# Layer 0's product with w_out: weight columns move, intermediates stand; its output in token rows

## The chip, the cores and the metric

One core of one Trainium2 chip runs the whole program. The metric is device time in microseconds (us), as the median of three runs. The engines are PE (matrix products; its weight loads are listed apart as PEld), DVE and ACT (element-wise work), POOL (element-wise work that can't read PSUM) and SP, whose queue issues nearly all DMA transfers. They run side by side, each in its own fixed order, and wait for each other by semaphores.

## What is computed

Causal attention with a forget bias for 4 x 8 heads of 576 tokens, then two feed-forward layers over the 2304 tokens. Model width is 512, inner width 2048.

```python
attn_out = _attn_ref(**attn_kwargs)                      # [4, 8, 576, 64]
x = attn_out.transpose(0, 2, 1, 3).reshape(B * S, H * D)  # [2304, 512]

# layer 0
h = x @ w_in
r = np.maximum(h, 0.0)
g = s * (r * r) + b          # s, b: one number each
x = g @ w_out

# layer 1
h = x @ w_in
g = np.maximum(h, 0.0) + alpha * np.minimum(h, 0.0)
return g @ w_out
```

Since b is one number, b's part of layer 0's result is b times the column sums of w_out, the same row for every token. The kernel calls it `bsum`.

## The kernel before

**Precision.** Every operand of a matmul is split into a high and a low part (`split`, L129: ACT copies the source rounded, DVE or POOL subtracts). A product is three matmuls: high x high, high x low, low x high. The weights come as 64-bit numbers and are rebuilt to 32 bits by one ACT and two DVE instructions (`convert`, L134) before they are split.

**Blocks.** Tokens go in blocks of T = 256. `SIZES` (L621) gives layer 0 seven narrow blocks of 256 tokens (t = 0 to 6) and a wide one of 512 (t = 7). Layer 1 has one narrow block (t = 0) and then four wide ones. A block is 16 steps f, one for each 128 of the inner width. `up(f)` (L699) makes 128 inner values for all its tokens: 12 matmuls into `hp`, the weights stationary, the tokens moving. ACT, DVE or POOL then make the high and low part `gh` and `gl` (in wide blocks and in layer 1 they lie in `ring`, `gl`'s part written at L131). `down(f)` (L740) multiplies by w_out and adds into the accumulators `acc`. `down` runs 2 steps behind `up` in layer 0 and 3 behind in layer 1 (`LAG`). `finish` (L761) takes the accumulators out through `res`.

**The two forms of down.** In layer 0 (L746) a 128x128 piece of w_out is stationary and `gh` or `gl` moves: 4 pieces x 3 terms = 12 matmuls a step, of 256 columns in a narrow block and 512 in the wide one. The result has the model's columns on the partitions and tokens along the row, as `up` of the next layer needs it. In layer 1 (L756) 128 tokens of `gh` or `gl` are stationary and the 512 columns of w_out move: 3 matmuls for each 128 tokens, 6 a step in the narrow block and 12 in a wide one. The result has tokens on the partitions, as the output needs it.

**Between the layers.** Layer 0's `finish` scales and adds `bsum` (L772, L776: a bias for each partition) and stores to the DRAM tile `x2_d`, which keeps the turned form. `inputs(1, t)` loads it as it lies (L636 for the narrow block, L657 for wide ones: 4 loads of 256 KB) and splits it. `sum_columns` (L233) makes `bsum` with 32 matmuls near the end of layer 0's first block, when all its weights are there.

**Attention** runs beside layer 0's narrow blocks. It is cut into units; `pace` says how many units must be done by which step, and the units' pieces are issued between the steps. Its loads of q and k (L323) bring pieces of 32 columns (128 B) to 32 partitions each, and DVE turns every 32x32 square (`nc.vector.transpose`, L371).

**Order.** Within the program order as written a scheduler moves instructions on each engine by its own estimate of times. SP's queue is in order, and at most 8 of its transfers are on the way at once.

Of the kernel before, what the change touches and what calls it, by code (L numbers as in the profile page):

```python
# [19 lines left out]
def tile_forget_attention__then__two_mlps(  # L20
# [597 lines left out]
    x2_d = dram.tile([NB, P, NCC * T], F32, name="x2_d")  # L618
# [3 lines left out]
    BLOCKS = [(layer, t) for layer in range(2) for t in range(len(SIZES[layer]))]  # L622

    def inputs(layer, t):
# [4 lines left out]
        if layer == 0:  # L629
            src = xf.pop(t)  # L630
            xh = one.tile([P, NCC, T], F32R, tag=f"xh{t % 2}", name=f"xh{layer}_{t}")
            xl = one.tile([P, NCC, T], F32R, tag=f"xl{t % 2}", name=f"xl{layer}_{t}")
            xh, xl = ([x[:, c] for c in range(NCC)] for x in (xh, xl))
        else:
            src = one.tile([P, NCC, T], F32, tag="res", name=f"x2_{t}")
            nc.sync.dma_start(out=src, in_=x2_d[t].rearrange("p (c n) -> p c n", n=T))  # L636

            xh, xl = (
                [
                    two.tile([P, T], F32R, tag=tag, name=f"x{tag}{layer}_{t}_{c}", bufs=3 if c < 3 else 2)  # L640
                    for c, tag in enumerate(tags)
                ]
                for tags in (("gh", "gh", "gh", "r"), ("gl", "gl", "gl", "r"))
            )
        for c in range(NCC):
            on_pool = layer == 0 and t
            split(xh[c], xl[c], src[:, c], nc.gpsimd if on_pool else nc.vector)
        return xh, xl

    def wide_inputs(layer, t, first):  # L650
        xh, xl = [], []
        src = []
        for half in range(2):
            if layer == 1:
                src.append(xfp.tile([P, 2, 2, T], F32, tag="xf", name=f"x2_{t}_{half}"))
                for z in range(2):
                    nc.sync.dma_start(  # L657
                        out=src[half][:, :, z],
                        in_=x2_d[first + z, :, half * 2 * T : (half + 1) * 2 * T].rearrange("p (c n) -> p c n", n=T),
                    )  # L660
# [14 lines left out]
        for c in range(NCC):  # L675
            if layer == 1:
                split(xh[c], xl[c], src[c // 2][:, c % 2].rearrange("p z n -> p (z n)"))
# [9 lines left out]
    def mlp_block(layer, t, x):  # L687
# [52 lines left out]
        def down(f, g):  # L740
            w = packet(layer, f)
            if layer == 0:
                terms = ((w[2], g[0]), (w[3], g[0]), (w[2], g[1]))
                for d in range(NCC):
                    for n, (a, b) in enumerate(terms):
                        nc.tensor.matmul(  # L746
                            banks[d] if count == 2 else acc[d // 2][:, d % 2], a[:, d * P : (d + 1) * P], b,
                            start=(f == 0 and (d % 2 == 0 or count == 2) and n == 0),
                            stop=(f == NF - 1), skip_group_check=True,
                        )  # L750
            else:
                gh, gl = g
                _, _, woh, wol = w
                for m in range(TB // P):
                    for a, b in ((gh, woh), (gh, wol), (gl, woh)):
                        nc.tensor.matmul(  # L756
                            banks[m], a[:, m * P : (m + 1) * P], b,
                            start=(f == 0 and b is woh and a is gh), stop=(f == NF - 1 and a is gl),
                        )

        def finish():  # L761
            for m, bank in enumerate(banks):
# [4 lines left out]
                if layer == 0:  # L767
                    for z in range(1 if count == 2 else 2):
                        d = m if count == 2 else 2 * m + z
                        dst, src = (res, bank) if count == 2 else (x[:, z * T : (z + 1) * T] for x in (res, bank))  # L770
                        if d % 2:
                            nc.scalar.activation(  # L772
                                dst, src, AF.Identity, scale=gate_s[:, 0:1], bias=bsum[:, d : d + 1]
                            )
                        else:
                            nc.vector.tensor_scalar(  # L776
                                out=dst, in0=src, scalar1=gate_s[:, 0:1], scalar2=bsum[:, d : d + 1],
                                op0=ALU.mult, op1=ALU.add,
                            )
                elif m % 2:  # L780
                    nc.scalar.mul(res, bank, 1.0 / W_SCALE)
                else:
                    nc.vector.tensor_scalar(out=res, in0=bank, scalar1=1.0 / W_SCALE, scalar2=None, op0=ALU.mult)
                if layer == 0 and count == 2:
                    nc.sync.dma_start(
                        out=x2_d[first : first + 2, :, m * T : (m + 1) * T].rearrange("z p n -> p z n"),
                        in_=res.rearrange("p (z n) -> p z n", n=T),
                    )
                elif layer == 0:
                    nc.sync.dma_start(out=x2_d[t, :, m * 512 : (m + 1) * 512], in_=res)  # L790
                else:
                    p0 = first * T + m * P
                    nc.sync.dma_start(out=out[p0 : p0 + P, :], in_=res)
# [98 lines left out]
```

## Time and profile before

| | |
|---|---|
| runs | 1047.58, 1049.14, 1053.61 us |
| median | 1049.14 us |
| span of the profiled execution | 1046.3 us |
| PE busy, matmuls | 1031.2 us, 6376 |
| PEld busy | 910.3 us |
| DVE busy | 584.2 us |
| ACT busy | 625.9 us |
| POOL busy | 340.6 us |
| mean DMA rate | 80 GB/s |

The profile is of one execution. Its span runs from the first to the last instruction and lies a little under the times of the runs. PE's busy time says little, since matmuls are pipelined and their ends are modelled; the distance from one start to the next, or a count in a stretch, says more. The stages of the span are: attention with the weights' arrival and layer 0's first block (to about 170 us), attention beside layer 0's other narrow blocks (to about 556), layer 0's wide block, in which layer 1's weights are loaded and converted (to about 650), layer 1's narrow block (to 689), and its wide blocks.

### The profile page before, as it was taken

What the parts mean: (1) busy time and instruction counts of PE and PEld (TensorE: products, weight loads), DVE (VectorE), ACT (ScalarE), POOL (GpSimd) and SP (SyncE); (2) the same over time, 40 slices, a digit from 0 to 9 for tenths busy, and PEclk for the clock granted to TensorE, in tenths of its full rate; (3) what the DMA queues carried; (4) which work ended last, traced back from release to release, by engine and by line L of the source; (5) the groups of instructions that cost most, each with busy time, mean ns of one, the idle gap of its engine ahead of it and who ended that gap; (6) DMA issues with size and microseconds to landing.
All of it is one profiled execution on the core that took longest, in us unless ns stands there. A gap on an engine that the chain in (4) does not pass through costs nothing.

```text
span 1046.3 us, 18413 instructions
## 1 busy us (share of the span) xinstructions
PE 1031.2 (99%) x6376; PEld 910.3 (87%) x6376; DVE 584.2 (56%) x1437; ACT 625.9 (60%) x1493; POOL 340.6 (33%) x752
## 2 busy tenths in 40 slices
PE   9899999999999999999999999999999999999998
PEld 4578899999999999999998888988888888888887
DVE  6789776687667766767655766532223224222222
ACT  5778766877787877878776766542334324333232
POOL 5344565766677566777550000000000000000000
PEclk9899999999999999999999999999999999999999
DMA  6998433243133332324215742300002002001001
GB/s 133 241 236 247 129 76 72 71 96 78 39 89 70 95 79 44 86 63 90 63 54 178 243 162 88 94 21 1 1 1 81 1 1 81 1 0 41 1 1 41
DMA packets 173470, 83.36 MB, mean 80 GB/s; under 512 B 135552, under 2 KB 160896, under 8 KB 173376
## 3 DMA queue, kind: packets, MB, share of 16 engines
q1 hardware_dynamic: 171984, 81.94, 29.8%
q8 instruction: 50, 0.82, 0.3%
q10 hardware_dynamic: 1392, 0.24, 0.1%
q14 instruction: 44, 0.36, 0.1%
HBM read 72.63 MB, written 9.51 MB: 79 GB/s over the span
## 4 chain that ended last, share of the span: by engine, by line
PE 84%; DVE 6%; DMA 3%; issue 2%; ACT 2%; SPq 2%; POOL 1%; DVEq 0%; POOLq 0%; ACTq 0%
PE hp L710 35%; PE acc L756 19%; PE acc L746 17%; PE pt L511 4%; PE av L527 4%; PE sc L456 2%; PE sc L455 1%; DMA wo<-in_moe_w_out_dram 1%; DVE probs L431 1%; SPq L323 1%; PE sc L453 1%; DVE probs L457 1%; DVE wt L142 1%; DMA cum<-cum_d 1%; PE colsum L241 1%
## 5 line engine op out<-in xcount | busy, mean ns | idle before, releaser
L710 PE MATMUL hp<-xh,w 128*128 128x256 f32 (+1 forms) x1536 | 397.3, 330 | 2.3 <-ACT r L729 1.5
L710 PEld LDWEIGHTS hp<-xh,w 128*128 128x128 f32 x1536 | 267.5, 189 | 31.1 <-ACT r L729 1.8
L710 PE MATMUL hp<-xl,w 128*128 128x256 f32 (+1 forms) x768 | 252.7, 329 | 0.3 <-DVE xl L131 0.3
L729 ACT ACTIVATE r<-hp 128x256 f32<-128x256 f32 (+1 forms) x208 | 96.5, 464 | 226.3 <-PE hp L710 214.7
L756 PE MATMUL acc<-w,ring 128*128 128x512 f32 x864 | 209.0, 390 | 0.0
L756 PEld LDWEIGHTS acc<-w,ring 128*128 128x128 f32 x864 | 161.3, 188 | 33.3
L746 PE MATMUL acc<-gh,w 128*128 128x256 f32 x896 | 169.9, 286 | 0.4 <-ACT res L772 0.3
L734 DVE SCALAR_TENSOR_TENSOR r<-u,misc,r 128x512 f32<-128x512 f32 (+1 forms) x80 | 55.8, 698 | 200.5 <-ACT u L733 200.5
L710 PEld LDWEIGHTS hp<-xl,w 128*128 128x128 f32 x768 | 145.2, 189 | 13.2 <-DVE xl L131 0.5
L746 PEld LDWEIGHTS acc<-gh,w 128*128 128x128 f32 x896 | 135.3, 189 | 2.9 <-ACT res L772 1.0
L746 PE MATMUL acc<-gl,w 128*128 128x256 f32 x448 | 117.6, 287 | 2.0 <-POOL gl L131 2.0
L480 POOL TENSOR_SCALAR probs<-probs,sm 64x64 f32<-64x64 f32 (+4 forms) x160 | 91.9, 587 | 63.7 <-DVE sm L477 56.4
L469 ACT ACTIVATE probs<-probs,nm 64x64 f32<-64x64 f32 (+4 forms) x160 | 90.0, 563 | 32.4 <-DVE nm L457 26.8
L131 POOL TENSOR_TENSOR gl<-r,gh 128x256 fp32r<-128x256 f32 x112 | 89.2, 797 | 61.8 <-ACT gh L130 55.6
L131 DVE TENSOR_TENSOR ring<-r,ring 128x512 fp32r<-128x512 f32 (+1 forms) x96 | 62.1, 647 | 60.9 <-ACT ring L130 60.9
L457 DVE CUSTOM_DVE_ANT_0 probs<-sc,probs 128x320 f32<-128x320 f32 (+3 forms) x160 | 68.3, 428 | 44.6 <-PE sc L456 31.4
L130 ACT CAST ring<-r 128x512 fp32r<-128x512 f32 (+1 forms) x96 | 56.0, 584 | 53.3 <-DVE r L734 52.7
L746 PEld LDWEIGHTS acc<-gl,w 128*128 128x128 f32 x448 | 79.8, 188 | 3.4 <-POOL gl L131 2.6
L511 PE MATMUL pt<-ident,probs 128*128 128x128 f32 x480 | 76.2, 278 | 2.8 <-POOL probs L480 2.8
L545 DVE TENSOR_TENSOR xf<-av,xf 64x128 f32<-64x128 f32 (+3 forms) x88 | 28.0, 318 | 67.7 <-ACT xf L544 67.2
L511 PEld LDWEIGHTS pt<-ident,probs 128*128 128x128 f32 x480 | 55.5, 141 | 9.4 <-POOL probs L480 4.4
L431 DVE TENSOR_SCALAR probs<-cum,cumT 64x64 f32<-64x64 f32 (+4 forms) x137 | 57.5, 468 | 5.6 <-issue 2.0
(116 smaller groups left out, 1557.8 us busy)
## 6 DMA issues: line engine op xcount, KB each, us to landing
wi<-in_moe_w_in_dram SPq DMA_DIRECT2D x32, 512.0 KB, 5.1
wo<-in_moe_w_out_dram SPq DMA_DIRECT2D x32, 512.0 KB, 4.9
cum<-cum_d SPq DMA_DIRECT2D x32, 288.0 KB, 3.5
cum<-cum_d SPq DMA_DIRECT2D x30, 160.0 KB, 3.1
nat<-in_k_dram SPq DMA_DIRECT2D x64, 72.0 KB, 2.5
x_d<-res SPq DMA_DIRECT2D x18, 256.0 KB, 2.2
out_dram<-res SPq DMA_DIRECT2D x18, 256.0 KB, 2.1
vn<-in_v_dram SPq DMA_DIRECT2D x32, 128.0 KB, 2.9
```

Of the source, the lines that this page charges most:

```text
L130: nc.scalar.copy(hi, src)
L131: lo_eng.tensor_tensor(out=lo, in0=src, in1=hi.bitcast(F32), op=ALU.subtract)
L431: nc.vector.tensor_scalar(out=pt[:rows, :i1], in0=u.cums[h][:rows, :i1], scalar1=cumT[:rows, r, head : head + 1], scalar2=0.0, op0=ALU.sub ...
L457: nc.vector.tensor_tensor_reduce(out=pt[:rows, j0:j1], in0=scr, in1=pt[:rows, j0:j1], scale=SCALE if flip else -SCALE, scalar=init, op0=AL ...
L469: nc.scalar.activation(pt[:rows, :n], pt[:rows, :n], AF.Exp, bias=nm[:rows, m : m + 1], scale=1.0 if flip else -1.0, accum_out=sm[:rows, m ...
L480: nc.gpsimd.tensor_scalar(out=probs[r][:rows, :n], in0=probs[r][:rows, :n], scalar1=sm[:rows, m : m + 1], scalar2=1.0, op0=ALU.mult, op1=A ...
L511: nc.tensor.transpose(tp[:, o : o + P], u.probs[h][r][:, k0 : k0 + P], ident)
L710: nc.tensor.matmul(hs, a[:, c], b[c], start=(n == 0), stop=(n == len(terms) * NCC - 1))
L729: relus.append(nc.scalar.activation(r, hs, AF.Relu, scale=1.0 / W_SCALE).ins)
L734: nc.vector.scalar_tensor_tensor(out=r, in0=u, scalar=nalpha[:, f : f + 1], in1=r, op0=ALU.mult, op1=ALU.add)
L746: nc.tensor.matmul(banks[d] if count == 2 else acc[d // 2][:, d % 2], a[:, d * P : (d + 1) * P], b, start=(f == 0 and (d % 2 == 0 or count ...
L756: nc.tensor.matmul(banks[m], a[:, m * P : (m + 1) * P], b, start=(f == 0 and b is woh and a is gh), stop=(f == NF - 1 and a is gl),)
```

## The change

Layer 0's `down` takes layer 1's form: `gh` and `gl` are stationary, w_out's 512 columns move. `finish` becomes one for both layers, with only a scale, and `x2_d` holds token rows. `inputs(1, t)` brings them back to the turned form: `load_rows` loads pieces of 32 columns with the pattern of q and k, 4 loads for each 128 columns, DVE turns the 32x32 squares, and `split_biased` adds `bsum` while it splits. A narrow block's load is 16 transfers in place of 1, a wide one's 16 in place of 4.

```diff
-    x2_d = dram.tile([NB, P, NCC * T], F32, name="x2_d")
+    x2_d = dram.tile([NT, DM], F32, name="x2_d")
+    def load_rows(dst, t0, n, c):
+
+        for g in range(4):
+            nc.sync.dma_start(
+                out=dst[32 * g : 32 * (g + 1)].rearrange("p (b d) -> p b d", d=32),
+                in_=x2_d[t0 : t0 + n, c * P + 32 * g : c * P + 32 * (g + 1)].rearrange("(b p) d -> p b d", p=32),
+            )
+
+    def split_biased(hi, lo, src, c):
+        nc.scalar.activation(hi, src, AF.Identity, bias=bsum[:, c : c + 1])
+        nc.vector.scalar_tensor_tensor(
+            out=lo, in0=src, scalar=bsum[:, c : c + 1], in1=hi.bitcast(F32), op0=ALU.add, op1=ALU.subtract
+        )
...
-            src = one.tile([P, NCC, T], F32, tag="res", name=f"x2_{t}")
-            nc.sync.dma_start(out=src, in_=x2_d[t].rearrange("p (c n) -> p c n", n=T))
+            rows = one.tile([P, NCC, T], F32, tag="res", name=f"x2_{t}")
+            for c in range(NCC):
+                load_rows(rows[:, c], first * T, T, c)
...
+            turned = one.tile([P, T], F32, tag=("ql00", "ql10", "ql11")[c % 3], name=f"x2t_{t}_{c}")
+            nc.vector.transpose(turned, rows[:, c])
+            split_biased(xh[c], xl[c], turned, c)
...
-                src.append(xfp.tile([P, 2, 2, T], F32, tag="xf", name=f"x2_{t}_{half}"))
-                for z in range(2):
-                    nc.sync.dma_start(
-                        out=src[half][:, :, z],
-                        in_=x2_d[first + z, :, half * 2 * T : (half + 1) * 2 * T].rearrange("p (c n) -> p c n", n=T),
-                    )
+                rows = xfp.tile([P, 4 * T], F32, tag="xf", name=f"x2_{t}_{half}")
+                for c in range(2):
+                    load_rows(rows[:, c * 2 * T : (c + 1) * 2 * T], first * T, 2 * T, 2 * half + c)
+                src.append(rows)
...
-                split(xh[c], xl[c], src[c // 2][:, c % 2].rearrange("p z n -> p (z n)"))
+                if c % 2 == 0:
+                    turned = xfp.tile([P, 4 * T], F32, tag="xf", name=f"x2t_{t}_{c}")
+                    nc.vector.transpose(turned, src[c // 2])
+                split_biased(xh[c], xl[c], turned[:, c % 2 * 2 * T : (c % 2 + 1) * 2 * T], c)
...
-            w = packet(layer, f)
-            if layer == 0:
-                terms = ((w[2], g[0]), (w[3], g[0]), (w[2], g[1]))
-                for d in range(NCC):
-                    for n, (a, b) in enumerate(terms):
-                        nc.tensor.matmul(
-                            banks[d] if count == 2 else acc[d // 2][:, d % 2], a[:, d * P : (d + 1) * P], b,
-                            start=(f == 0 and (d % 2 == 0 or count == 2) and n == 0),
-                            stop=(f == NF - 1), skip_group_check=True,
-                        )
...
+            gh, gl = g
+            _, _, woh, wol = packet(layer, f)
+            for m in range(TB // P):
+                for a, b in ((gh, woh), (gh, wol), (gl, woh)):
+                    nc.tensor.matmul(
+                        banks[m], a[:, m * P : (m + 1) * P], b,
+                        start=(f == 0 and b is woh and a is gh), stop=(f == NF - 1 and a is gl),
+                    )
...
+                scale = gate_s[:, 0:1] if layer == 0 else 1.0 / W_SCALE
+                if m % 2:
+                    nc.scalar.mul(res, bank, scale)
                 else:
-                    nc.vector.tensor_scalar(out=res, in0=bank, scalar1=1.0 / W_SCALE, scalar2=None, op0=ALU.mult)
...
+                    nc.vector.tensor_scalar(out=res, in0=bank, scalar1=scale, scalar2=None, op0=ALU.mult)
+                p0 = first * T + m * P
+                nc.sync.dma_start(out=(x2_d if layer == 0 else out)[p0 : p0 + P, :], in_=res)
```

Three places show what the scheduler makes of it. The first is PE in layer 0's narrow block 3, at the down of step 4 (w_4_2_18 and w_4_2_17 are the high and low part of w_out there; pt, sc and av are attention). Before:

```order
L746 MATMUL acc_3_0_4704<-gh_3_4_5018,w_4_2_18_912 128x256
L746 MATMUL acc_3_0_4704<-gh_3_4_5018,w_4_2_17_913 128x256
L746 MATMUL acc_3_1_4705<-gh_3_4_5018,w_4_2_18_912 128x256
L746 MATMUL acc_3_1_4705<-gh_3_4_5018,w_4_2_17_913 128x256
L511 MATMUL pt_0_2_1_0_4852<-ident,probs_1_0_1_4741 128x128 x3
L455 MATMUL sc_1_0_2_2_0_4862<-xs_2_2_0_4774 128x192
L456 MATMUL sc_1_0_2_2_0_4862<-xs_2_2_0_4774,ql_113 128x192
```

After:

```order
L765 MATMUL acc_3_0_4424<-w_4_2_18_912,gh_3_4_4712 128x512
L765 MATMUL acc_3_0_4424<-w_4_2_17_913,gh_3_4_4712 128x512
L765 MATMUL acc_3_1_4425<-w_4_2_18_912,gh_3_4_4712 128x512
L765 MATMUL acc_3_1_4425<-w_4_2_17_913,gh_3_4_4712 128x512
L765 MATMUL acc_3_0_4424<-w_4_2_18_912,gl_3_4_4713 128x512
L765 MATMUL acc_3_1_4425<-w_4_2_18_912,gl_3_4_4713 128x512
L730 MATMUL hp_3_6_4916<-xh_3_4067,w_6_0_24_1233 128x256
```

The twelve of the step, of which the first four stand above, became six, and the two with `gl`, which POOL writes last, stand at their end.

The second is DVE in layer 1's narrow block, around steps 4 to 8 (r and ring belong to a step's intermediates; x_1 and x_2 are the next two wide blocks' inputs in two halves each). Before:

```order
L734 SCALAR_TENSOR_TENSOR r_0_5_10175<-u_0_5_10176,misc,r_0_5_10175 128x256
L131 TENSOR_TENSOR xl_2_0_10813<-x_2_0_10809,xh_2_0_10812 128x512 x2
L131 TENSOR_TENSOR ring_9986<-r_0_5_10175,ring_9982 128x256
L734 SCALAR_TENSOR_TENSOR r_0_6_10201<-u_0_6_10202,misc,r_0_6_10201 128x256
L131 TENSOR_TENSOR xl_2_1_10818<-x_2_1_10814,xh_2_1_10817 128x512 x2
L131 TENSOR_TENSOR ring_9987<-r_0_6_10201,ring_9983 128x256
```

After (x2t is the turned form):

```order
L131 TENSOR_TENSOR ring_9323<-r_0_5_9512,ring_9319 128x256
L696 STREAM_TRANSPOSE x2t_2_9683<-x_1_1_9666 128x1024
L754 SCALAR_TENSOR_TENSOR r_0_6_9538<-u_0_6_9539,misc,r_0_6_9538 128x256
L634 SCALAR_TENSOR_TENSOR xl_1_1_9676<-x2t_2_9683,misc,xh_1_1_9675 128x512 x2
L754 SCALAR_TENSOR_TENSOR r_0_7_9564<-u_0_7_9565,misc,r_0_7_9564 128x256
L131 TENSOR_TENSOR ring_9324<-r_0_6_9538,ring_9320 128x256
L131 TENSOR_TENSOR ring_9325<-r_0_7_9564,ring_9321 128x256
L696 STREAM_TRANSPOSE x2t_0_10184<-x_2_0_10162 128x1024
L754 SCALAR_TENSOR_TENSOR r_0_8_9590<-u_0_8_9591,misc,r_0_8_9590 128x256
L634 SCALAR_TENSOR_TENSOR xl_2_0_10172<-x2t_0_10184,misc,xh_2_0_10171 128x512 x2
L131 TENSOR_TENSOR ring_9322<-r_0_8_9590,ring_9318 128x256
```

The work on x_2 moved from steps 5 and 6 to steps 8 and 9, and the turn of its first half stands ahead of r and ring of step 8. Its loads use the buffers that the turns of x_1 free.

The third is ACT in layer 0's first block, between steps 2 and 4 (wt_7, wt_8: weight packets being rebuilt; w_6, w_7: split; probs and pf: attention). Before:

```order
L469 ACTIVATE probs_1_1_0_986,sm_1_1_0_985<-probs_1_1_0_986,nm_1_1_0_984 128x448
L130 CAST gh_0_2_1218<-r_2_1220 128x256
L130 CAST w_7_0_28_1285<-wt_7_0_1277 128x512
L515 COPY pf_0_1_1_0_1006<-pt_0_0_0_1_1001 128x512
L469 ACTIVATE probs_1_1_0_986,sm_1_1_0_985<-probs_1_1_0_986,nm_1_1_0_984 128x576
L427 ACTIVATE probs_1_1_1_1045<-cum_0_1_1_973,cumT 128x448
L427 ACTIVATE probs_1_1_1_1045<-cum_0_1_1_973,cumT 128x576
L729 ACTIVATE r_3_1272<-hp_0_3_1257 128x256
L140 ACTIVATE wt_8_0_1329<-wi_8_1241 128x512
L140 ACTIVATE wt_8_1_1333<-wo_8_1242 128x512
```

After:

```order
L469 ACTIVATE probs_1_1_0_986,sm_1_1_0_985<-probs_1_1_0_986,nm_1_1_0_984 128x448
L130 CAST w_7_0_28_1279<-wt_7_0_1271 128x512
L749 ACTIVATE r_3_1266<-hp_0_3_1251 128x256
L140 ACTIVATE wt_8_0_1317<-wi_8_1241 128x512
L140 ACTIVATE wt_8_1_1321<-wo_8_1242 128x512
L130 CAST w_7_2_30_1283<-wt_7_1_1275 128x512
L751 ACTIVATE r_3_1266<-r_3_1266 128x256
L515 COPY pf_0_1_1_0_1006<-pt_0_0_0_1_1001 128x512
L427 ACTIVATE probs_1_1_1_1045<-cum_0_1_1_973,cumT 128x448
L427 ACTIVATE probs_1_1_1_1045<-cum_0_1_1_973,cumT 128x576
```

Step 3 and packet 8 moved ahead of four pieces of attention; DVE's order changed alike, up to packet 14.

## Rows read from the trace of the kernel before

**Rows 1.** Page, busy time, share of the span and instructions of each engine.

```profile
PE 1031.2 (99%) x6376; PEld 910.3 (87%) x6376; DVE 584.2 (56%) x1437; ACT 625.9 (60%) x1493; POOL 340.6 (33%) x752
```

**Rows 2.** Stretches: us, busy PE PEld DVE ACT POOL (count), clock, DMA share, GB/s.

```profile
50.00:100.00 50.00, 47.21 (x299) 38.18 (x299) 46.13 (x107) 39.22 (x94) 22.34 (x33) 1.00 0.94 252
300.00:350.00 50.00, 50.00 (x420) 49.94 (x419) 35.71 (x114) 40.26 (x117) 36.70 (x90) 1.00 0.33 74
720.00:1020.00 300.00, 300.00 (x1322) 247.81 (x1321) 88.06 (x124) 101.53 (x179) 0.00 (x0) 1.00 0.05 18
```

**Rows 3.** Chain of waits, narrow block, layer 0: start us, us, what, instructions.

```profile
402.75 1.66 PE acc L746 x14
...
442.74 1.43 PE hp L710 x12
```

**Rows 4.** PE by form, layer 0's down: count, busy us, mean ns, idle before.

```profile
L746 PE MATMUL acc<-gh,w 128*128 128x256 f32 x896 | 169.9, 286 | 0.4 <-ACT res L772 0.3
...
L746 PE MATMUL acc<-gl,w 128*128 128x256 f32 x448 | 117.6, 287 | 2.0 <-POOL gl L131 2.0
```

**Rows 5.** Chain of waits, layer 1's narrow block.

```profile
661.14 1.44 PE hp L710 x12
662.58 1.40 PE acc L756 x6
```

**Rows 6.** Chain of waits, wide blocks of layer 0 (L746) and layer 1 (L756).

```profile
606.87 2.79 PE acc L746 x12
...
726.53 2.72 PE acc L756 x12
```

**Rows 7.** Tile acc: layer 0's evictions, ns min/median/max; then who waited (us, times).

```profile
L776 DVE TENSOR_SCALAR res<-acc,misc x16: 505/530/809, 169.7 to 652.0; 128x256 f32<-128x256 f32 x14, 128x512 f32<-128x512 f32 x2
L772 ACT ACTIVATE res<-acc,misc x16: 547/558/777, 170.6 to 653.2; 128x256 f32<-128x256 f32 x14, 128x512 f32<-128x512 f32 x2
...
  PEld acc L746: 1.0, 3
  PE acc L746: 0.3, 2
```

**Rows 8.** DMA: issues with KB each and median us to landing; packets by size.

```profile
DMA packets 173470, 83.36 MB, mean 80 GB/s; under 512 B 135552, under 2 KB 160896, under 8 KB 173376
...
nat<-in_k_dram SPq DMA_DIRECT2D x64, 72.0 KB, 2.5
...
x<-x_d SPq DMA_DIRECT2D x16, 256.0 KB, 4.6
```

**Rows 9.** Line 323, SP's issue of one load of k, ns min/median/max.

```profile
L323 SPq DMA_DIRECT2D nat<-in_k_dram x112: 311/461/2185, 45.1 to 486.9; - x112
```

**Rows 10.** Lines 371, 131, 734 on DVE, ns min/median/max: turn, low part, two operations.

```profile
L371 DVE STREAM_TRANSPOSE turned<-nat x29: 823/1026/1045, 5.4 to 498.9; 128x832 f32<-128x832 f32 x16, 128x640 f32<-128x640 f32 x13
...
L131 DVE TENSOR_TENSOR xl<-x,xh x16: 684/688/694, 658.5 to 885.7; 128x512 fp32r<-128x512 f32 x16
...
L734 DVE SCALAR_TENSOR_TENSOR r<-u,misc,r x80: 474/752/756, 645.0 to 1033.0; 128x512 f32<-128x512 f32 x64, 128x256 f32<-128x256 f32 x16
```

**Rows 11.** Timeline of DVE, layer 1's narrow block, rings of steps 5 and 8.

```profile
664.23 0.42 DVE L131 TENSOR_TENSOR ring<-r,ring 128x256 fp32r<-128x256 f32 x1
...
670.01 0.43 DVE L131 TENSOR_TENSOR ring<-r,ring 128x256 fp32r<-128x256 f32 x1 [0.47 <-ACT ring L130]
```

**Rows 12.** Timeline of PE, the same block, down of step 8.

```profile
676.62 1.56 PE L756 MATMUL acc<-w,ring 128*128 128x512 f32 x6
```

**Rows 13.** Chain of waits from 60 to 110 us; line 140's waits (us, times).

```profile
76.29 6.84 DMA wi<-in_moe_w_in_dram
...
93.40 6.83 DMA wo<-in_moe_w_out_dram
...
  DMA wi<-in_moe_w_in_dram: 5.5, 5
...
  DMA wo<-in_moe_w_out_dram: 1.8, 3
```

More of the change, by code (lines that the diff above doesn't have):

```diff
@@ L645, in inputs @@
         for c in range(NCC):
-            on_pool = layer == 0 and t
-            split(xh[c], xl[c], src[:, c], nc.gpsimd if on_pool else nc.vector)
+            if layer == 0:
+                split(xh[c], xl[c], src[:, c], nc.gpsimd if t else nc.vector)
+                continue
+            turned = one.tile([P, T], F32, tag=("ql00", "ql10", "ql11")[c % 3], name=f"x2t_{t}_{c}")
+            nc.vector.transpose(turned, rows[:, c])
+            split_biased(xh[c], xl[c], turned, c)
         return xh, xl
@@ L740, in down @@
         def down(f, g):
-            w = packet(layer, f)
-            if layer == 0:
-                terms = ((w[2], g[0]), (w[3], g[0]), (w[2], g[1]))
-                for d in range(NCC):
-                    for n, (a, b) in enumerate(terms):
-                        nc.tensor.matmul(
-                            banks[d] if count == 2 else acc[d // 2][:, d % 2], a[:, d * P : (d + 1) * P], b,
-                            start=(f == 0 and (d % 2 == 0 or count == 2) and n == 0),
-                            stop=(f == NF - 1), skip_group_check=True,
-                        )
[L751 to L759, printed above, removed]
+            gh, gl = g
[6 more added lines that the diff above has]
+                    )
         def finish():
@@ L766, in finish @@
                 res = both[:, m % 2 * 512 : (m % 2 + 1) * 512]
[L767 to L781, printed above, removed]
-                else:
-                    nc.vector.tensor_scalar(out=res, in0=bank, scalar1=1.0 / W_SCALE, scalar2=None, op0=ALU.mult)
[L784 to L793, printed above, removed]
+                scale = gate_s[:, 0:1] if layer == 0 else 1.0 / W_SCALE
+                if m % 2:
+                    nc.scalar.mul(res, bank, scale)
+                else:
+                    nc.vector.tensor_scalar(out=res, in0=bank, scalar1=scale, scalar2=None, op0=ALU.mult)
+                p0 = first * T + m * P
+                nc.sync.dma_start(out=(x2_d if layer == 0 else out)[p0 : p0 + P, :], in_=res)
         return up, down, finish
```

## The prediction

> **What bounds the kernel now.** I read the page's busy times first, then the table by stretches, then the chain of waits in three places, and only then single tiles. TensorE (PE) has work for 99% of the span [rows 1], but that busy time is partly modelled, so the count of matmuls in a stretch tells more. From 300 to 350 us, inside layer 0's narrow blocks, 420 matmuls fill 50 us, and the weight loads (PEld) are busy for 49.94 of them; DVE and ACT have about 14 and 10 us free there [rows 2]. That is 0.119 us a matmul, although those of the attention move 64, 128 or 320 columns. In this stage the engine takes one stationary operand every 0.119 us, whatever moves over it: 12 up matmuls of 256 columns take 1.43 us and 14 down matmuls 1.66 us, with no other engine between them in the chain [rows 3]. In layer 1 the wide blocks run at 1322 matmuls in 300 us, PEld busy for 247.81 of them [rows 2]: with 512 columns moving, the moving side is the limit. The clock is granted in full (1.00, 2.4 GHz) in all these stretches. Only the first 150 us are different: from 50 to 100 us PE starts 299 matmuls, DVE is busy for 46.13 of 50 us and DMA moves 252 GB/s at a share of 0.94 [rows 2]. What counts, therefore, is PE's own work after about 150 us, and everything else only where it makes PE wait.
>
> **Removed and added on PE, narrow blocks.** Seven blocks of 16 steps lose 1344 down matmuls of 256 columns [rows 4] and get half as many of 512. A step's twelve cost 12 x 1.66/14 = 1.42 us, or 1.43 at the pitch of the up group [rows 3]. The new six exist in the trace already: layer 1's first block has 256 tokens, and its step is twelve ups of 256 and six downs of 512 with the intermediate stationary. There the six take 1.40 us and the twelve ups 1.44 [rows 5]. So a step goes from 1.43 to 1.40: 0.03 us, times 7 x 16 = 112 steps, is **3.4 us** less. The columns streamed are the same (12 x 256 = 6 x 512), which is why halving the matmuls gives so little. Bounds: if the ups behind the wider matmuls go at 1.44 for 1.43, 0.02 us a step or 2.2 us is left. If the six go at the pitch of the wide blocks, 2.72/2 = 1.36 [rows 6], it is 0.07 a step or 7.8 us. A loss is excluded by the rows: the slowest 512-column pitch among them, 1.40/6 = 0.233 us, is under two 256-column ones, 0.238. I take 3.4, since rows 5 show the same step, operand for operand.
>
> The Trainium skill speaks of this too. The page "TensorE: Matmul & The Clock Gate", section "Back-to-back issue gap", gives for a real kernel's stream of load and matmul pairs a sustained 131 ns a matmul at 512 columns. By that the estimate for a step's six is 0.79 us, 0.64 less than now, and for the sum 72 us less. The trace differs: 0.227 us in the longest undisturbed stream [rows 6], and the measurement decides.
>
> **The wide block of layer 0** (16 steps of twelve 512-column downs) swaps which operand is stationary. Its twelve take 2.79 us now; layer 1's wide blocks, which do what the change makes of it, 2.72 [rows 6]. 16 x 0.07 = **1.1 us**. The bounds are 0 (the pitch belongs to the place, not to the operands) and 1.1; I take 1.1, as the rows differ in just this.
>
> **Eviction.** A narrow block ends with two DVE and two ACT instructions of 256 columns (0.53 and 0.56 us each); they become one of 512 each, without the bias. PE and PEld wait for the ACT ones 1.3 us in all, five times [rows 7]. So between 0 and 1.3 us; I take 0, since the first bank comes free no sooner. The first block's eviction also no longer waits for the column sums; the sums still run on PE, so nothing is gained while PE has other work.
>
> **Loads of layer 1.** 17 loads become 80: 16 for the narrow block and 16 for each of four wide ones, in pieces of 128 B. Each wide one carries 64 KB. The nearest row is the load of k, with the same 32-column pattern: 72 KB land 2.5 us after issue [rows 8], and SP needs 0.461 us to issue one [rows 9]. Sixteen take 7.4 us to issue, and the last lands near 10 us, where four loads of 256 KB landed 4.6 us after issue each [rows 8]. On SP only the stores of results are queued behind them, and nobody waits for those. The narrow block's loads go out among the fetches of layer 1's weights, which are used a stage later. The later wide blocks have steps of twice 2.72 us [rows 6] and three steps between an up and its down: 16 us, so they hide it. Cost 0 there.
>
> **DVE and ACT.** Two turns of 128x1024 come with each wide block. A turn of 128x832 took 1.026 us [rows 10], so an estimated 1.26 us: 10 us in all, over 300 us in which DVE was busy for 88 [rows 2]. The biased split replaces a subtraction of 0.688 us by a two-operation form that took 0.752 on 512 columns [rows 10]: 16 x 0.06 = 1 us, hidden likewise. If that cover were gone, 11 us would be the price. The tight place is layer 1's first block, with steps of 2.84 us. In the new order DVE must turn the second wide block's first half (x_2_0) before it may finish r and ring of step 8. Those loads can start when x_1_1 has been turned, about 665.9 us on the old clock: the ring of step 5 ends at 664.65 [rows 11] and the turn takes 1.26. Eight issues (3.7), the landing (2.5) and the turn bring 673.4. The r (0.5), two low parts (1.5, with ACT's high parts ahead of them) and the ring (0.4) end near 676, against 670.44 before [rows 11]. Step 8's down group starts at 676.62 and needs the low part with its third matmul, 677.1 [rows 12]. So it just fits, with 1 us to spare: **0**, up to 3 us if it doesn't.
>
> **The first 150 us.** The new order lets DVE and ACT convert weight packets 7 to 14 ahead of attention work that stood before them. DVE's work is the same, and DMA sets when a packet can be converted at all. I take 0. The ends are a gain of 3.9 us, which is what DVE had free from 50 to 100 us [rows 2], and a loss of 13.7 (below).
>
> **Sum.** 3.4 + 1.1 = 4.5 us off the profiled span of 1046.3 us gives 1041.8. The median of the three runs, 1049.14, lies 2.8 us above that span (the fastest, 1047.58, 1.3 above). Carried to the median: **1044.6 us**, 0.43% faster. About 0.5%, or 5.2 us, is what a measurement of this kernel can tell from no change, so the forecast itself stands just inside "same".
>
> **Rivals.**
> - *The six go at the wide pitch.* 7.8 + 1.1 = 8.9 us: **1040.2 us**. For it: the wide stages with 512 columns throughout hold 0.227 us. Against: layer 1's first block mixes widths just as the new step does, and holds 0.233.
> - *Slower: DVE stands at a weight packet.* DVE works strictly in its order. If a conversion that now stands ahead of attention work comes before its packet has landed, the attention work behind it, and PE behind that, wait. The price of one landing is 6.8 us (two such pieces stand in the chain [rows 13]). One gives 1051.4; two give 1044.6 + 13.7 = **1058 us**. It turns the result from 4.5 us of such waits on. For it: DMA's share of 0.94 leaves loads no room to come sooner. Against: the moves are by about one packet, and ACT, which converts first, has waited for weight packets only 5.5 + 1.8 us in the whole kernel [rows 13].
> - *The turn of x_2_0 comes late.* If 64 KB in small pieces land like the old 256 KB loads, 4.6 us for 2.5 [rows 8], the spare microsecond is gone and PE waits 1 to 1.5 us at steps 8 and 9: 1 to 3 us, **1046 to 1048 us**. The Trainium skill's page "DMA: Bandwidth & Descriptors", section "Specifications", wants 512 B for full rate and so speaks against these pieces. The row of k's load shows no such loss at this size.
> - *The skill's 131 ns a matmul holds in the narrow steps.* PE would then be free and the next engine would bound the stage. That is ACT with 40.26 of 50 us [rows 2], so the 400 us from 150 to 550 could shrink to 322 at best: about **971 us**. No 512-column row is under 0.226 us, so this has under 1 chance in 100.
>
> **Chances.** Forecast 0.57: 0.20 of it beyond 0.5% faster (early stretch or evictions add a microsecond), 0.37 within. Wide pitch 0.18, all faster. Late weight packets 0.15: 0.06 within 0.5%, 0.09 slower. Late turn 0.10, within. That is 0.38 faster, 0.53 same, 0.09 slower. The range goes from 1039.5 (wide pitch and a little more) to 1051 (one late packet); it leaves out the second packet.
>
> **What the new profile would show.** Matmuls 6376 - 672 = 5704. In the chain of a narrow step, six downs at 1.40 us (1.36 if the rival is right) beside twelve ups at 1.43 or 1.44. PEld below 47 of 50 us there. Layer 0's wide downs at 2.72 per twelve. Packets under 512 B up by 4 x 8192 + 4096 = 36864, to 172416. In layer 1's first block DVE idle for some 3 us before the turn of x_2_0, but no gap on PE. The late-packet rival would show as idle time of DVE or ACT ending on wi or wo before 130 us, and the first eviction of a block later than 170 us. I am wrong if the down group isn't near 1.40 us, or if PE has gaps around 670 to 680 us or many more before 150 us than now.

## The result and the profile after

The changed kernel takes **1057.14 us** (median of 8 runs, 1053.48 to 1060.02) where the kernel before takes 1047.54 (8 runs). The ratio of the means is **1.0078, interval 1.0054 to 1.0102**: slower by 0.5 to 1.0%. The forecast was 0.43% faster, the range ended at 1051, and slower had a chance of 0.09.

The profiled execution took 1056.49 us. Its span and the engines' busy times (to be read beside [rows 1]):

```profile
span 1054.7 us, 17157 instructions
...
PE 1031.4 (98%) x5704; PEld 876.1 (83%) x5704; DVE 593.2 (56%) x1442; ACT 626.4 (59%) x1486; POOL 342.1 (32%) x752
```

The matmuls are as many as predicted, 5704. The span is 8.4 us longer and PE's busy time 0.2 us: span less busy time, which is PE's idle time, went from 15.1 to 23.3 us. So PE does not work longer, **it stands longer**. Where it does is seen from the start of the first eviction of each block (us, from the trace):

| block | t=0 | 1 | 2 | 3 | 4 | 5 | 6 | wide | layer 1 narrow | last |
|---|---|---|---|---|---|---|---|---|---|---|
| before | 169.7 | 226.3 | 297.2 | 360.8 | 430.7 | 494.7 | 568.0 | 650.9 | 701.3 | 1040.7 |
| after | 151.2 | 222.3 | 298.9 | 363.3 | 434.2 | 501.5 | 576.2 | 659.2 | 709.6 | 1049.0 |
| difference | -18.5 | -4.0 | +1.7 | +2.5 | +3.5 | +6.8 | +8.2 | +8.3 | +8.3 | +8.3 |

The first entry comes from the column sums, which no longer stand ahead of that eviction. All of the loss arises in the narrow blocks t=2 to t=6; the wide block and all of layer 1 add 0.1 us. Where PE stands shows it too: its waits are 1.6 us more before 150 us (9.1 for 7.5), 6.8 us more from 150 to 580, and none behind that. What PE waited for from 150 to 580 us (engine, line, releaser: us in total, times, longest), first in the kernel before:

```profile
PE hp L710 <- ACT r L729: 1.5, 2, 0.8
PE acc L746 <- POOL gl L131: 1.4, 2, 1.0
PE acc L746 <- ACT res L772: 0.3, 2, 0.2
PE av L527 <- DVE pl L131: 0.2, 1, 0.2
```

and after:

```profile
PE hp L730 <- ACT xh L130: 3.4, 1, 3.4
PE hp L730 <- ACT r L749: 2.5, 4, 1.0
PE av L527 <- DVE pl L131: 1.7, 2, 1.0
PE hp L730 <- POOL xl L131: 1.3, 2, 0.9
PE pt L511 <- POOL probs L480: 0.9, 1, 0.9
PE acc L765 <- ACT gh L130: 0.4, 1, 0.4
```

3.4 us became 10.2. The long one is an up that waits for the high part of its block's tokens. The chain of waits there (start, us, what):

```profile
222.27 0.52 ACT res L778
222.79 0.19 issue
222.98 0.31 ACT xf L544
223.29 0.02 issue
223.31 0.62 ACT vs_all L130
223.93 0.79 ACT xs L389
224.72 0.66 ACT probs L469 x2
225.38 0.02 issue
225.41 0.26 ACT xf L544
225.66 0.02 issue
225.69 0.41 ACT xh L130
226.10 0.04 issue
226.14 0.58 PE hp L730
```

The last attention product for block t=2's tokens ends on PE near 222.7 us. Its result still has to be copied (L544) and split (L130), and on ACT an eviction, two casts and a softmax step stand in between. The next instruction on PE is the up that needs it. PE's order of the changed kernel at that place (av: the attention product; hp_2_0: step 0 of block t=2, the fourth of its four groups of three ups), where nothing is left between them:

```
L527 MATMUL av_1_3_0_2931<-pl_3_0_1_0_2939,vs_all 128x192
L527 MATMUL av_1_3_0_2931<-ph_3_0_1_1_2957,vs_all 128x64
L527 MATMUL av_1_3_0_2931<-pl_3_0_1_1_2958,vs_all 128x64
L730 MATMUL hp_2_0_3339<-xh_2_2983,w_0_0_0_176 128x256
L511 MATMUL pt_0_1_0_1_3115<-ident,probs_0_1_0_2916 128x128
```

Counted for the blocks t=1 to 6, the order before had 27, 46, 32, 47, 32 and 46 matmuls between that product and the first of the three ups that read it; the new order has 0, 0, 16, 11, 16 and 17. At the pitches of the trace (a pitch is the distance from one matmul's start to the next) that is 3.2 to 5.8 us against 0 to 2.6. The distance is not all: with none at t=1 either, PE waited only 0.9 us there (at 146.5 us).

The long wait has a second price. The granted clock (last column but two) in stretches of 5 us, after the wait:

```profile
220.00:225.00 5.00, 2.73 (x16) 2.15 (x14) 4.94 (x14) 3.55 (x7) 2.27 (x6) 0.99 0.33 73
225.00:230.00 5.00, 3.86 (x16) 3.74 (x17) 2.47 (x7) 2.77 (x7) 3.42 (x6) 0.50 0.70 133
230.00:235.00 5.00, 4.71 (x31) 4.20 (x30) 3.90 (x10) 4.06 (x11) 2.87 (x5) 0.83 0.49 166
235.00:240.00 5.00, 5.00 (x37) 4.62 (x36) 3.08 (x10) 3.40 (x10) 2.15 (x5) 1.00 0.00 0
```

In the kernel before the same stretches have 1.00 throughout; the second of them:

```profile
225.00:230.00 5.00, 4.87 (x39) 4.76 (x40) 3.55 (x11) 3.10 (x10) 2.61 (x4) 1.00 0.39 129
```

0.50 is the lower of the two levels, 1.2 GHz. By the clock, 0.50 of 3.86 us and 0.17 of 4.71 are lost there, 2.7 us.

### The profile page after: what moved, and what is told of

It is laid out like the page before. It is cut to its first block, busy times and chain, and to the rows that moved or that the text cites. A ratio compares the mean times of both kernels' runs of the same rounds, so it can differ in the third digit from the quotient of the medians.

```text
span 1054.7 us, 17157 instructions
## 1 busy us (share of the span) xinstructions
PE 1031.4 (98%) x5704; PEld 876.1 (83%) x5704; DVE 593.2 (56%) x1442; ACT 626.4 (59%) x1486; POOL 342.1 (32%) x752
## 2 busy tenths in 40 slices
DMA packets 206602, 83.28 MB, mean 79 GB/s; under 512 B 173425, under 2 KB 193649, under 8 KB 206513
## 4 chain that ended last, share of the span: by engine, by line
PE 90%; DMA 3%; ACT 3%; SPq 2%; DVE 1%; issue 1%; POOL 1%; POOLq 0%; ACTq 0%; DVEq 0%
PE hp L730 38%; PE acc L765 37%; PE av L527 5%; PE pt L511 5%; PE sc L456 2%; PE sc L455 2%; PE sc L453 1%; SPq L323 1%; DMA vn<-in_v_dram 1%; DMA wo<-in_moe_w_out_dram 1%; PE colsum L241 1%; ACT probs L469 1%; DMA cum<-cum_d 0%; DMA nat<-in_k_dram 0%; SPq L332 0%
## 5 line engine op out<-in xcount | busy, mean ns | idle before, releaser
L765 PE MATMUL acc<-w,ring 128*128 128x512 f32 x1056 | 256.4, 391 | 0.0
L765 PEld LDWEIGHTS acc<-w,ring 128*128 128x128 f32 x1056 | 197.4, 188 | 41.5
L765 PE MATMUL acc<-w,gh 128*128 128x512 f32 x448 | 133.5, 403 | 1.1 <-ACT gh L130 0.4
L765 PEld LDWEIGHTS acc<-w,gh 128*128 128x128 f32 x448 | 77.8, 189 | 12.9 <-ACT r L749 0.7
L130 ACT CAST ring<-r 128x512 fp32r<-128x512 f32 (+1 forms) x96 | 55.9, 584 | 52.8 <-DVE r L754 52.3
L765 PE MATMUL acc<-w,gl 128*128 128x512 f32 x224 | 76.5, 401 | 0.0
L435 POOL TENSOR_SCALAR_AFFINE_SELECT probs<-probs 128x128 f32<-128x128 f32 (+1 forms) x160 | 54.7, 366 | 27.8 <-DVE probs L431 12.0
```

Of the source, the lines that this page charges most:

```text
L130: nc.scalar.copy(hi, src)
L435: nc.gpsimd.affine_select(out=pt[:rows, i0:i1], in_=pt[:rows, i0:i1], pattern=[[-1, rows]], base=0, channel_multiplier=1, compare_op=ALU.i ...
L765: nc.tensor.matmul(banks[m], a[:, m * P : (m + 1) * P], b, start=(f == 0 and b is woh and a is gh), stop=(f == NF - 1 and a is gl),)
```

## The experiments

Two theories. **Order**: the wider downs are as cheap as predicted, but the order that the scheduler builds around them lets PE run into operands that aren't there yet. Its first wording, called "reserve" in the first expectations, was narrower: the distance between a block's last attention product and its first use is too short. **Form or width**: swapped operands, turned loads, biased split, or 512-column matmuls among attention's cost the time themselves. "Idle" is span less PE's busy time in the one profile of each kernel. Runs of one kernel spread with the granted clock (the kernel before: 1045.75 to 1058.40 us); over 167 runs of these eleven kernels one slope fits, 0.75 us for each 0.001 of mean clock, and the last column carries the mean of each kernel to a clock of 0.995 by it (with its 95% interval). The ratio is to the runs of the kernel before that were made beside each.

| kernel | ratio to before, interval | idle, us | at clock 0.995, us |
|---|---|---|---|
| before | 1 | 15.1 | 1050.4 ± 0.3 |
| changed | 1.0078, 1.0054 to 1.0102 | 23.3 | 1056.4 ± 0.8 |
| halves | 1.0011, 0.9991 to 1.0031 | 18.3 | 1052.8 ± 0.7 |
| narrow_old | 1.0015, 0.9983 to 1.0048 | 17.5 | 1052.9 ± 0.7 |
| edge15 | 1.0064, 1.0041 to 1.0087 | 21.3 | 1055.4 ± 0.8 |
| edge14 | 1.0077, 1.0047 to 1.0107 | 26.0 | 1057.8 ± 1.0 |
| wide_old_order | 1.0024, 0.9998 to 1.0050 | 19.1 | 1052.0 ± 0.7 |
| halves_new_order | 1.0106, 1.0069 to 1.0143 | 23.8 | 1060.4 ± 1.0 |
| pe_before_order | 1.0018, 0.9990 to 1.0046 | 19.5 | 1051.7 ± 0.7 |
| all_before_order | 1.0010, 0.9988 to 1.0032 | 17.9 | 1049.2 ± 0.7 |
| pe_prefix | 1.0004, 0.9981 to 1.0027 | 18.5 | 1050.6 ± 0.7 |

**halves**: everything as changed, the narrow downs in twelve pieces.

```diff
-                for a, b in ((gh, woh), (gh, wol), (gl, woh)):
-                    nc.tensor.matmul(
-                        banks[m], a[:, m * P : (m + 1) * P], b,
...
+                for z in range(2 if layer == 0 and count == 1 else 1):
+                    cols = slice(z * T, (z + 1) * T) if layer == 0 and count == 1 else slice(0, 512)
+                    for a, b in ((gh, woh), (gh, wol), (gl, woh)):
+                        nc.tensor.matmul(
+                            banks[m][:, cols], a[:, m * P : (m + 1) * P], b[:, cols],
...
```

> The changed kernel, but each narrow step's six down matmuls of 512 columns are written as twelve of 256 (same operands, same result). On PE this brings back an order in which, between the last attention product for a block's tokens and the three ups of that block's step 0 that need it, stand 3.1 to 5.8 us of other matmuls; in the changed kernel there are 0 to 2.6. Theory 'reserve' (the changed order lets PE run into x before it is copied, added and split; some 6 us of waits at block starts and some 3 us of lowered clock after the longest): no wait over 1 us on PE at a block's start between 200 and 510 us, clock 1.00 from 220 to 240 us, 1047 to 1050 us. Rival 'form' (the swapped operands, the turned loads or the biased split cost the time): 1055 to 1058 us, since all of these are still there.

The ratio is 1.0011 (median 1051.94 us beside 1050.59, so above the 1047 to 1050 that "reserve" gave). PE waits nowhere for `xh` after 150 us; its longest wait at block t=2 is 1.15 us, for a bank that ACT still reads, with the clock at 1.00 behind it. Operands, layout, turned loads, biased split and evictions are all as changed, so **none of them costs the 0.8%**. One microsecond of what is left was not expected: in the wide block PE stood once for a low part that DVE made late, since a turn of layer 1's input stood ahead of it and waited for its load. PE's waits in halves from 585 to 600 us:

```profile
PE acc L767 <- DVE ring L131: 1.0, 1, 1.0
```

and DVE's in the same stretch:

```profile
DVE x2t L665 <- DMA x<-x_d: 3.3, 2, 2.9
```

**narrow_old**: the old form in the narrow blocks alone.

```diff
+            if layer == 0 and count == 1:
+                w = packet(layer, f)
+                for d in range(NCC):
+                    for n, (a, b) in enumerate(((w[2], g[0]), (w[3], g[0]), (w[2], g[1]))):
+                        nc.tensor.matmul(acc[d // 2][:, d % 2], a[:, d * P : (d + 1) * P], b, ...
+                return
             gh, gl = g
```

> The changed kernel with the old form of down (w_out stationary, twelve matmuls of 256 columns) in the narrow blocks alone; wide block, eviction, stores, turned loads and biased split stay as changed, so layer 1 gets the narrow blocks' results in the wrong layout (same amount of work). PE's order is that of the run named halves. Theory 'reserve': 1047 to 1050 us, the same as halves within 1 us. Rival 'form' with the loss in layer 1's loads or in the wide block: still 1055 us or more. Rival 'form' with the loss in the narrow blocks' swapped operands: 1047 to 1049 here, but 1055 or more in halves.

1.0015, and the same as halves at equal clock (1052.9 and 1052.8, each ± 0.7): which operand is stationary makes no difference that these runs show at equal width, and with layer 1's loads and the wide block as changed the loss is gone here too.

**edge15** and **edge14**: a rule of order that keeps a distance between the last product and its use.

```diff
...
-        late.append((down, finish, f, up(f)))
+        with tc.issue_after(avs[goal - 1]) if layer == 0 and f == 15 and t < NB - 2 else nullcontext():
+            late.append((down, finish, f, up(f)))
```

(avs holds each unit's last attention product; edge14 has 14 for 15 and `LEAD` 6 for 4.)

> The changed kernel with one rule of order more: in layer 0 PE may issue the ups of a block's step 15 only after the last attention product that the next block needs. That puts 2.5 to 5.6 us of matmuls between that product and its first use (0 to 2.6 in the changed kernel), with nothing else changed. Theory 'reserve': most of the waits at block starts go, 1047 to 1051 us. Rival 'form': 1056 to 1058 us.

> As edge15, but the rule holds for step 14 and attention is paced 6 steps ahead of a block for 4, which puts 5.6 to 7.3 us of matmuls between the last product and its use. Theory 'reserve' with the narrow steps' gain of 0.03 us each as predicted: no wait over 0.5 us on PE at a block's start after 150 us, and 1044 to 1048 us, at or below the kernel before. If attention moved ahead costs as much as it saves: 1050 to 1056 us. Rival 'form': 1056 us or more.

Both miss: 1.0064 and 1.0077, near where the rival "form" put them; it is halves that excludes this rival. The wait for `xh` is gone, but others take its place. In edge15 two of them, 2.3 us for POOL at 219.9 us and 1.9 us for DVE at 223.9, stand close together, and the clock falls behind them as well (the column of the clock has 0.66):

```profile
225.00:230.00 5.00, 5.00 (x31) 4.94 (x30) 3.57 (x12) 4.79 (x11) 4.43 (x6) 0.66 0.44 71
```

PE's waits in edge14 from 150 to 580 us:

```profile
PE hp L731 <- ACT r L750: 5.8, 6, 1.2
PE pt L511 <- POOL probs L480: 3.0, 2, 2.1
PE av L527 <- DVE pl L131: 1.5, 3, 0.5
```

Two steps' ups now stand back to back, and the second waits for its bank until ACT has read it. So the theory in its first wording falls: **the distance at the block's start is not the whole of it**. What was left was the order as a whole, and whether width costs something in any order. The next three tell that apart.

**wide_old_order** and **halves_new_order**: the orders exchanged. Both kernels have the same instructions except the narrow downs, so each can be given the other's order.

```diff
+    for name, runs in ORDER.items():
+        engine, ops = KINDS[name]
+        of = [i for i in nc.cur_bb.bb.instructions if i.engine == getattr(nc, engine).engine and i.opcode in ops]
+        todo = [of[k] for first, n in runs for k in range(first, first + n)]
...
+        for a, b in zip(todo, todo[1:]):
+            tc.add_manual_dep(
+                b, a.name, mybir.DependencyInfo(mybir.DependencyClass.NoSync, mybir.DependencyReason.DATA), reason="order"
+            )
...
+ORDER = {"PE":[[0,48],[50,2],
...
```

> The changed kernel, instruction for instruction, with its order on PE, DVE, ACT, POOL and SP written out by hand: it is the order that the run named halves had, with each pair of 256-column halves replaced by its one matmul of 512 columns. Theory 'order' (the loss is the order that the scheduler chose for the wider matmuls): the time of halves (1.001 of before) less the predicted 3.4 us of the narrow steps, so 1045 to 1050 us on a chip where before takes 1048 to 1050, a ratio of 0.997 to 1.001. Rival 'width' (512-column downs among attention's matmuls cost the time in whatever order): a ratio of 1.006 to 1.010, as the changed kernel has.

> The converse: the twelve 256-column downs of the run named halves, with the order of the changed kernel on all five engines, written out by hand (each matmul of 512 columns replaced by its two halves). Theory 'order': the waits at block starts come back (3 us at one, about 1 us at five), and the ratio to before is 1.007 to 1.012, the changed kernel's 1.008 plus up to the 3.4 us that twelve narrow downs take longer. Rival 'width': 1.001, as halves has.

| at clock 0.995, us | order of halves | order of the changed kernel | the order costs |
|---|---|---|---|
| twelve of 256 | 1052.8 | 1060.4 | 7.6 ± 1.2 |
| six of 512 | 1052.0 | 1056.4 | 4.4 ± 1.1 |
| the six save | 0.9 ± 1.0 | 4.1 ± 1.3 | |

**The order costs 4 to 8 us with either width; the width itself costs nothing that these runs show, and saves in one of the two orders.** The converse run, at 1.0106 within what was expected of it, shows the wait again, without any 512-column down in a narrow block (one of PE's waits from 150 to 580 us in halves_new_order):

```profile
PE hp L730 <- ACT xh L130: 3.4, 1, 3.4
```

and the clock behind it, in the same table of stretches as above:

```profile
225.00:230.00 5.00, 4.22 (x17) 3.97 (x18) 2.47 (x8) 2.69 (x6) 3.16 (x6) 0.51 0.69 130
230.00:235.00 5.00, 4.71 (x34) 4.42 (x33) 3.62 (x9) 4.04 (x12) 3.15 (x5) 0.81 0.45 165
```

wide_old_order came out above what was expected, 1.0024 for at most 1.001: in an order made for twelve, the six bring 0.9 us of their 3.4 (idle 19.1 us against 18.3). Its interval ends at 1.0050, below the rival's 1.006.

**pe_before_order** and **all_before_order**: the changed kernel with the order of the kernel before, on PE alone and on all five engines, by the same edit with other lists.

> The changed kernel with PE's order alone written out by hand: that of the kernel before, with each pair of 256-column downs of the narrow blocks replaced by one matmul of 512 columns. The other engines are ordered by the scheduler around it. Theory 'order': 1.1 us of the gaps of halves go too, and what is left is the pitch: 3.4 us of gain in the narrow blocks and 0.6 us of loss in the wide one (its twelve go at 2.80 for 2.79 us and its ups at 2.76 for 2.73 in the changed kernel), so a ratio of 0.995 to 0.999, the fastest of all. Rival 'width': 1.006 or more. If DVE's or ACT's order matters as much as PE's: 1.002 to 1.006.

> The changed kernel with the order of the kernel before written out by hand on PE, DVE, ACT, POOL and SP, for every instruction that both have (of each pair of narrow evictions on an engine one stands for both; the turns, the biased splits and the added loads of layer 1 are free). Theory 'order': PE's idle time falls from the changed kernel's 23 us (span less PE's busy time) to the 15 to 16 us of the kernel before, and what is left is the pitch, 3.4 us gained in the narrow blocks and 0.6 us lost in the wide one: a ratio of 0.996 to 0.999. If a part of the loss is still in the operands or the layout, 1.001 to 1.005, as with PE's order alone.

Both ratios are above what theory "order" gave, and 1.0010 lies at the edge of what the expectation gave to a loss left in operands or layout. With PE's order alone 4.4 us of idle time more than before are left; the orders of the other engines matter too. Near 297 and 432 us a down waited about 1 us for its operands while ACT did an eviction first. With all five engines the idle time is 17.9 us and not 15 to 16: 2.6 us more than before stand ahead of 170 us, 1.7 of them in one wait for a load of v. At equal clock the kernel is 1.2 us faster than before (1049.2 ± 0.7 against 1050.4 ± 0.3); the ratio, 1.0010 with an interval of 0.0022 to either side, does not tell that from no change or from a small loss. PE's own time decides it better. The page of all_before_order:

```profile
span 1044.7 us, 17160 instructions
...
PE 1026.8 (98%) x5700; PEld 873.0 (84%) x5704; DVE 597.2 (57%) x1442; ACT 627.3 (60%) x1486; POOL 342.1 (33%) x752
```

Between the evictions of t=1 and t=6, with as many attention matmuls (858) and nearly the same waits (2.1 us against 1.9), it takes 339.8 us where the kernel before takes 341.7: **0.4 us less a block**, where 16 x 0.03 = 0.48 was predicted.

**pe_prefix**: PE's order of before only up to 230 us.

> The changed kernel with PE's order fixed to that of the kernel before only from the start to the ups of step 1 of layer 0's third block (about 230 us); everything behind it is the scheduler's own. In what the scheduler then makes, 3.3 to 5.5 us of other matmuls stand between the last attention product and its use in the third, fourth and fifth blocks (0 to 2.6 in the changed kernel), 2.5 in the seventh. If the 3.4 us wait at 222 us and the lowered clock behind it are most of the loss: 1.001 to 1.004. If the small waits of the later blocks are most of it: 1.004 to 1.007.

1.0004, under both ranges and nearest to the one that makes the long wait most of the loss: PE's order of the first 230 us brings back nearly all. The wait of 3.4 us and the lowered clock behind it (2.7 us) are gone, together 6.1 us, where the kernel is 5.8 ± 1.1 us faster than the changed one at equal clock. Waits of about 1 us at the blocks behind stay. The edit also changed what the scheduler makes of the later blocks, so it doesn't price that wait alone.

**l1_load**: a look at the pitch of 512 columns (one run, 1057.88 us).

```diff
+            for _ in range(6 if layer == 1 and t in (1, 3) else 0):
+                nc.vector.tensor_scalar(out=u, in0=u, scalar1=1.0, scalar2=None, op0=ALU.mult)
+            for _ in range(4 if layer == 1 and t in (2, 3) else 0):
+                nc.scalar.copy(u, u)
             return gh, gl
```

> Only a look at the pitch of 512-column matmuls. In layer 1's wide blocks each step gets work that changes nothing: six more DVE passes over u in the first wide block, four more ACT passes in the second, both in the third, none in the fourth. In layer 0's wide block, with DVE and ACT busy, twelve take 2.76 to 2.80 us; in layer 1's wide blocks 2.72. If other engines' work slows the stream, the first three wide blocks show 2.74 to 2.82 a twelve and the fourth 2.72; if the pitch belongs to the tiles or their places, all four show 2.72. Total 1055 to 1062 us either way.

Neither came out as worded. In the first and third wide block (DVE loaded) the ups take 2.75 us and the downs 2.72; in the second (ACT loaded) and the fourth both take 2.72. The chain in the first:

```profile
730.78 2.72 PE acc L769 x12
733.50 2.75 PE hp L730 x12
```

and in the second:

```profile
815.35 2.72 PE hp L730 x12
818.07 2.72 PE acc L769 x12
```

DVE's six passes lengthen the ups by 0.03 us a twelve. That doesn't explain what the change did in layer 0's wide block: from 580 to 655 us DVE was busy for 52.2 us before and 52.4 after, and the ups took 2.73 and 2.76. The downs' 2.80 there aren't explained by it either; both stay open.

## Why the prediction was wrong, point by point

**Narrow steps, 3.4 us: right.** In the chain of the changed kernel around 332 us a step's six take 1.40 us beside twelve ups at 1.44, as in [rows 5]:

```profile
331.70 1.40 PE acc L765 x6
333.10 1.44 PE hp L730 x12
```

all_before_order confirms 0.4 us a block. The rival "wide pitch" (1.36) is out. One reading behind this term was wrong, though the sum doesn't use it: 0.119 us from matmul to matmul does not hold "whatever moves over it". It fits 256 columns and the mean of the stretch; in the kernel before, two of 448 columns take 0.20 us each from start to start:

```profile
222.82 0.37 PE L455 MATMUL sc<-xs 128*128 128x448 f32 x1
223.03 0.37 PE L456 MATMUL sc<-xs,ql 128*128 128x448 f32 x1
223.23 0.28 PE L710 MATMUL hp<-xl,w 128*128 128x256 f32 x1
```

**Wide block, 1.1 us: wrong in sign, small.** The swap gave 2.80 us a twelve for 2.79, and the ups behind it 2.76 for 2.73 ([rows 6] have 2.79 and 2.72 for the downs). The chain around 600 us, first the ups before, then both after:

```profile
604.14 2.73 PE hp L710 x12
...
598.36 2.80 PE acc L765 x12
601.16 2.76 PE hp L730 x12
```

16 x 0.04 = 0.6 us lost. The same 2.80 and 2.76 stand in halves, narrow_old and all_before_order, so they do not come from the order; the swap is what these kernels share, beside the turned loads and the biased split. The lower bound's reason, that the pitch belongs to the place, was the right one, and the bound should have gone below nothing: here the ups beside the swapped downs became slower too, for a reason that no run shows.

**Eviction, 0: right here.** PE's waits for an eviction from 150 to 580 us went from 0.3 us to none; in pe_before_order an eviction on ACT stood ahead of a down's operand twice, and PE waited 2 us, so the cover isn't certain. In the long wait at 222 us, too, an eviction is the first thing that ACT does, with 0.5 us.

**Loads and turns of layer 1, 0: right, with a wrong step on the way.** Packets under 512 B are 173425 (172416 predicted), a load of 64 KB lands 2.4 us after issue (2.5 taken from [rows 8]), the turn takes 1.25 us and the biased split's second part 0.75. PE has no gap from 650 us to the end. The rival "late turn" had its mechanism, but not in this kernel: in halves it cost 1.0 us. The group of those loads (KB each, median us to landing):

```profile
x<-x_d SPq DMA_DIRECT2D x64, 64.0 KB, 2.4
```

I expected DVE to stand some 3 us before the turn of x_2_0; it stood 0.5. The loads of x_2_0 began at 671.59 us, when the low parts of x_1_0 were done, and not when x_1_1 had been turned (673.93), so there was more room than worked out.

**The first 150 us, 0: the step that failed, in scope and in reading.** The time up to the second block's eviction is 4.0 us shorter, not equal, and the late-packet rival did not occur (ACT waited 3.7 us for wi and 1.4 for wo before 130 us, [rows 13] have 5.5 and 1.8). But the text stopped at 150 us: for waits of PE in the narrow blocks behind it the sum has no term, and there the runs show 6.8 us more of waits and 2.7 us of lowered clock. It had seen that the scheduler moves attention against the downs in the narrow blocks, and took for granted that what follows is "PE's own work after about 150 us, and everything else only where it makes PE wait", without asking whether it still doesn't. The 4.0 us at t=1 are for the most part attention put off, not time won: from there to t=6 PE runs 883 attention matmuls for 858, some 3 us more. And products put off arrive at a block's start just when they are needed. The numbers to see it by, 46 matmuls of distance against none, stood in the two orders before any run. None of the signs of being wrong that the prediction named points there either: the downs took 1.40 us, nothing gaped at 670 to 680 us, and the waits before 150 us grew by only 1.6 us.

**The sum.** Of the 8.4 us in the span, 8.2 are idle time. In PE's busy time four things nearly cancel: about -2.8 from the narrow steps (7 x 0.4, the figure of five blocks of all_before_order), +0.6 from the wide block, +2.7 from the lowered clock at 225 to 235 us, and about -1.6 because the early dip of the clock, which both kernels have, is 0.93 over one 25 us stretch for 0.86. That makes -1.1 where +0.2 was measured; 1.3 us are not accounted for. What in the order costs how much is shown for its first 230 us as a whole, not move by move, and why the scheduler chose it can't be read from a trace.

## What to carry to other kernels

Where a scheduler sets the order, a change of one instruction's length can change the whole order: before pricing the instruction, count on the bound engine what stands between each late product of the other engines and its first use, in the old order and in the new. A gain of 0.3% from the pitch is smaller than what such a reordering can take, so the order has to be held, or exchanged as here, before the change itself can be judged. And a wait that a single rule moved came back here under another name, twice (edge15, edge14), where the engines around PE are 60 to 80% busy.

## What the runs showed of the hardware

- A wait of 3.4 us on PE between busy stretches was followed in two kernels by 5 us at a granted clock of 0.50 and 0.51 and 5 us at 0.83 and 0.81; waits of up to 1.2 us at the same place in halves, wide_old_order and pe_before_order left it at 1.00, and so did one of 2.07 us in edge14 (at 221 us). In edge15 two waits of 2.3 and 1.9 us, four us apart, were followed by 5 us at 0.66. The wait of 3.4 us cost about 2.7 us more than it lasted.
- Run to run, the time of one and the same kernel follows the mean granted clock with 0.75 us for each 0.001 (one slope for 167 runs of eleven kernels); the kernel before ranges over 12.6 us. Differences of a few us between single profiles mean nothing without it.
- The pitch of a 512-column stream is not one number: twelve take 2.72 us in layer 1's wide blocks, 2.75 for the ups there with six DVE passes more a step (l1_load), and in layer 0's wide block 2.73 for ups beside 2.79 for downs before, 2.76 beside 2.80 after.
